# A DiT attention block on one core: x only centred for K, 1/sigma applied later, scale's first part of three blocks, w_mod by neighbouring rows

## The chip, the cores and the metric

The kernel runs on one NeuronCore of a Trainium2 chip. The core has a matrix engine (PE; its weight loads are listed apart as PEld), a vector engine (DVE), a scalar engine (ACT), a general-purpose engine (POOL) and a queue engine (SP), which here only issues transfers. ACT also issues a few. Transfers between the chip's DRAM (HBM) and the on-chip memory (SBUF) run on 16 DMA engines; matrix products land in a second on-chip memory (PSUM) of eight banks. The engines run side by side, each in its own order, and wait for one another through semaphores.

The metric is device time in microseconds of one execution. The kernel before takes 100.85 us, the median of three runs (100.76 to 101.13). Times in the text are us from the start of the profiled span unless a unit is given.

## The reference

The block is the attention half of a diffusion transformer with adaptive layer norm. B = 2 batches of N = 256 tokens, D = 1152, all bfloat16:

```
mod = (silu(c) @ w_mod).reshape(B, 6, 1, D)
shift_a, scale_a, gate_a, ... = [mod[:, i] for i in range(6)]
h = layernorm(x) * (1 + scale_a) + shift_a
q, k, v = split(h @ wqkv)
p = softmax(q @ k.T * D ** -0.5)
out = x + gate_a * ((p @ v) @ wo)
```

Three of the six modulation vectors are used: shift, scale and gate. `layernorm(x)` is `(x - mean) / sigma` per token, so 1/sigma is one number per token. Adding the same vector to every key adds, for one query, the same number to all its scores, which the softmax removes; so the shift may be left out of K.

## The kernel before, in words

D is cut into KT = 9 blocks of 128 and the 512 tokens into TT = 4 tiles of 128 (tiles 0 and 1 are batch 0, tiles 2 and 3 batch 1). Every engine's order is written out by hand: `vec`, `sca`, `ten` and `spq` record each DVE, ACT, PE and SP instruction (they all show as line L74 in the profile), and `pin` at the end fixes each engine's recorded order. POOL's instructions are not recorded and stand in program order. So the order of the source text is the order on each engine.

**Loads.** SP issues all weights and x in one sequence (L138 to L153): x tiles 1, 0, 3; the first KA x 128 columns of scale's weights (`wS`) in pairs of row blocks; K's rows 0 to KA - 1 (first 1024 columns, one row block each, with x tile 2 after the first); the rest of scale's columns; the rest of K's rows; K's last 128 columns of the first rows; shift's weights `wH`. Later come Q's and V's weights in chunks of 384 columns (`wqv`), the gate's weights `wG` and `wo`. c goes by ACT's queue (L118).

**c and the modulation.** c is loaded as 18 rows of 128 (L115, L118), turned by PE into `cT_ps` (L157), put through silu with one exponential on ACT and three DVE steps (`silu_c`, L170), and copied 27 times over by ACT into `scT_rep`, since a product with a few more columns is no dearer for PE. `scale_A`, `scale_B` and `shift_block` multiply blocks of `wS` and `wH` with it: scale's first KA = 4 blocks into `psSA` and `psS0` (which are started from ones, for 1 + scale), the other five into `psSB`, shift into `psH`. Twelve products on a constant (`fillers`, L160) run ahead of this on PE, seven more (`fillers2`, L256) between the first scale products and transposes.

**Layer norm.** For tiles 1, 0 and 2, DVE takes statistics (`dve_stats`, `dve_aggr`), POOL adds eps and raises to the power -0.5, DVE makes `nb` = -mean/sigma and then `xn` = x * rstd + nb in one step (`dve_norm`). For tile 3, ACT takes mean and variance (`act_mean`, `act_var`). PE turns `xn` block by block (`transposes`) and DVE or ACT copies the result to `xnT` (features on partitions, tokens along the row).

**K first.** K needs no shift, so it starts before shift is known: `scaled` (DVE) multiplies a block of `xnT` by 1 + scale into `hTs`; `k_part` adds a block of K's rows to six open accumulators (`accs`, one bank each, 512 tokens wide), first for batch 0 (256 columns), then tile 3, then tile 2 (128 columns each), for the first KA blocks; `early_half` does the same for two more output blocks, into `psE` and from there into `early`. Then come `scale_B`, `scaled` for the other blocks, and `k_step` for these with 512 columns. The accumulators are copied to `qkT` by DVE and ACT in turn (`evac`). Shift's products follow, with `k_block` for the remaining output blocks between them; DVE adds `early` to two of these, copies `psH` to `sh`, and `modulated` (DVE and ACT) makes `hT` = xnT * (1 + scale) + shift, the input of Q and V.

**Then** Q (nine blocks of nine products), the scores, softmax (`row_max`, `exps`, `normalized`), V, attention times V, and the output projection with the gate. The gate is summed on DVE in 18 steps (`gate_step`, `gacc`), reduced over partitions on POOL (`gate_bc`, L558), and POOL multiplies it into the last columns of `wo` (`wo_last`, L579), which PE's last products read.

Of the kernel before, what the change touches and what calls it, by code (L numbers as in the profile page):

```python
# [7 lines left out]
ACT = mybir.ActivationFunctionType  # L8
# [8 lines left out]
def kernel(  # L17
# [9 lines left out]
    nc = tc.nc  # L27
# [14 lines left out]
    KA = 4  # L42
# [6 lines left out]
    wmod_v = w_mod.rearrange("(kk p) (s n) -> p kk s n", p=P, s=6)  # L49
# [45 lines left out]
    def tok(b):  # L95
        return slice(b * N, (b + 1) * N)
# [13 lines left out]
    neg_half = const.tile([P, 1], F32)  # L110
# [4 lines left out]
    c_sb = const.tile([2 * KT, P], BF16)  # L115
    x_sb = act.tile([P, TT, D], BF16)
    nc.scalar.preload_act_table_set("natural_log_exp_and_others")
    nc.scalar.dma_start(out=c_sb, in_=c.rearrange("b (k p) -> (b k) p", p=P))  # L118
# [8 lines left out]
    def load_x(t):  # L127
        spq.dma_start(out=x_sb[:, t, :], in_=x_f[t * P : (t + 1) * P, :])

    def load_mod(tile_, which, k0, k1, c0, c1):  # L130
        spq.dma_start(out=tile_[:, k0:k1, c0:c1], in_=wmod_v[:, k0:k1, which, c0:c1])

    def load_k(k0, k1, c0=0, c1=D):
        spq.dma_start(out=wK[:, k0:k1, c0:c1], in_=wqkv_v[:, k0:k1, D + c0 : D + c1])
# [8 lines left out]
    load_k(0, 1, 0, WE)  # L143
    load_x(2)
    for k in range(1, KA):
        load_k(k, k + 1, 0, WE)
    load_mod(wS, 1, 0, 5, CA, D)
    load_mod(wS, 1, 5, KT, CA, D)
    load_k(KA, 6)
    load_k(6, KT)  # L150
# [5 lines left out]
    cT_ps = psum_b.tile([P, 2 * KT], BF16, tag="pb")  # L156
    ten.transpose(cT_ps, c_sb, ident[: 2 * KT, : 2 * KT])  # L157
    junk_ps = psum_a.tile([P, 512], F32, tag="pa")

    def fillers(n):  # L160
        for _ in range(n):
            ten.matmul(junk_ps, lhsT=ident, rhs=junk_rhs, start=True, stop=True)

    fillers(12)
    e_sb = small.tile([P, 2 * KT], F32, tag="e_sb")
    sca.activation(out=e_sb, in_=cT_ps, func=ACT.Exp, scale=-1.0)
# [3 lines left out]
    def silu_c():  # L170
        vec.tensor_scalar_add(out=e_sb, in0=e_sb, scalar1=1.0)
        vec.reciprocal(out=e_sb, in_=e_sb)
        vec.tensor_tensor(
            out=scT_f.rearrange("p k b -> p b k"),
            in0=cT_ps.rearrange("p (b k) -> p b k", b=B),
            in1=e_sb.rearrange("p (b k) -> p b k", b=B),
            op=ALU.mult,
        )
        sca.copy(out=scT_rep, in_=scT_f.unsqueeze(2).to_broadcast([P, KT, NR // B, B]))
# [5 lines left out]
    mv_all = const.tile([P, TT, 2], F32)  # L185
    rstd = const.tile([P, TT], F32)
    nb = const.tile([P, TT], F32)
    xn = act.tile([P, TT, D], BF16, tag="a1")
    xnT = act.tile([P, KT, T], BF16, tag="a2")
    stats = {t: small.tile([P, NCH, 6], F32, tag="stats", name="stats") for t in (1, 0, 2)}  # L190

    def dve_stats(t, s):
        vec.bn_stats(out=stats[t][:, s, :], in_=x_sb[:, t, s * CW : (s + 1) * CW])

    def dve_aggr(t):
        vec.bn_aggr(out=mv_all[:, t, :], in_=stats[t])
        nc.gpsimd.tensor_scalar_add(out=rstd[:, t : t + 1], in0=mv_all[:, t, 1:2], scalar1=EPS)
        nc.gpsimd.tensor_tensor(out=rstd[:, t : t + 1], in0=rstd[:, t : t + 1], in1=neg_half, op=ALU.pow)  # L198

    def dve_nb(t):  # L200
        vec.scalar_tensor_tensor(
            out=nb[:, t : t + 1], in0=mv_all[:, t, 0:1], scalar=-1.0, in1=rstd[:, t : t + 1],
            op0=ALU.mult, op1=ALU.mult,
        )

    def dve_norm(t):
        vec.tensor_scalar(
            out=xn[:, t, :], in0=x_sb[:, t, :], scalar1=rstd[:, t : t + 1], scalar2=nb[:, t : t + 1],
            op0=ALU.mult, op1=ALU.add,
        )  # L210

    ssum = small.tile([P, 1], F32, tag="ssum")
    nmean = small.tile([P, 1], F32, tag="nmean")
    ssq = small.tile([P, 1], F32, tag="ssq")

    def act_mean(t):
        sca.activation(out=xn[:, t, :], in_=x_sb[:, t, :], func=ACT.Copy, accum_out=ssum)
        sca.activation(out=nmean, in_=ssum, func=ACT.Copy, scale=-1.0 / D)

    def act_var(t):  # L220
        sca.activation(out=xn[:, t, :], in_=x_sb[:, t, :], func=ACT.Square, bias=nmean,
                       scale=1.0, accum_out=ssq)
        nc.gpsimd.tensor_scalar(out=rstd[:, t : t + 1], in0=ssq, scalar1=1.0 / D, scalar2=EPS,
                                op0=ALU.mult, op1=ALU.add)
        nc.gpsimd.tensor_tensor(out=rstd[:, t : t + 1], in0=rstd[:, t : t + 1], in1=neg_half, op=ALU.pow)
        nc.gpsimd.tensor_tensor(out=nb[:, t : t + 1], in0=nmean, in1=rstd[:, t : t + 1], op=ALU.mult)

    tps = {}
    HALF = ((0, KA), (KA, KT))

    def transposes(t, h, pool, tag):
        k0, k1 = HALF[h]
        tp = pool.tile([P, KB, P], BF16, tag=tag, name="tp")
        for k in range(k0, k1):
            ten.transpose(tp[:, k - k0, :], xn[:, t, k * P : (k + 1) * P], ident)
        tps[t, h] = tp

    def xnT_copy(t, h, on_dve):
        k0, k1 = HALF[h]
        dst, srct = xnT[:, k0:k1, t * P : (t + 1) * P], tps[t, h][:, : k1 - k0, :]  # L240
        if on_dve:
            vec.tensor_copy(out=dst, in_=srct)
        else:
            sca.copy(out=dst, in_=srct)

# [4 lines left out]
    hT = act.tile([P, KT, T], BF16)  # L250
    qkT = act.tile([P, 2 * KT, T], BF16)
    early = const.tile([P, NEARLY, T], F32)

    junk_mm = psum.tile([P, 512], F32, tag="mm")

    def fillers2(n):  # L256
        for _ in range(n):
            ten.matmul(junk_mm, lhsT=ident, rhs=junk_rhs, start=True, stop=True)
# [8 lines left out]
    def scale_A(kk):  # L267
        for j in range(KA):
            ten.matmul(
                psS0 if j == 0 else psSA[:, j - 1, :], lhsT=wS[:, kk, j * P : (j + 1) * P], rhs=sc_rhs(kk),  # L270
                start=False, stop=(kk == KT - 1), skip_group_check=True,
            )
# [15 lines left out]
    def one(t):  # L288
        return slice(t * P, (t + 1) * P)
# [11 lines left out]
    def early_half(k, b, ps):  # L301
        for i in range(NEARLY):
            ten.matmul(
                ps[:, i, :], lhsT=wK[:, k, (NACC + i) * P : (NACC + i + 1) * P], rhs=hTs[:, k, tok(b)],
                start=(k == 0 and i == 0), stop=(k == KA - 1), skip_group_check=True,
            )
# [19 lines left out]

    silu_c()
    for s in range(NCH):
        dve_stats(1, s)
    dve_aggr(1)  # L330
    for s in range(NCH):
        dve_stats(0, s)
    dve_aggr(0)
    act_mean(3)
    dve_nb(1)
    dve_norm(1)
    dve_nb(0)
    dve_norm(0)
    scale_A(0)
    fillers2(2)  # L340
    scale_A(1)
    fillers2(2)
    transposes(1, 0, psum, "mm")
    transposes(1, 1, psum, "mm")
    xnT_copy(1, 0, False)
    xnT_copy(1, 1, False)
    fillers2(3)
    scale_A(2)
    scale_A(3)
    transposes(0, 0, psum, "mm")  # L350
    transposes(0, 1, psum, "mm")
    xnT_copy(0, 0, True)
    xnT_copy(0, 1, True)
    act_var(3)
    for kk in range(4, KT):
        scale_A(kk)

# [8 lines left out]
    early_half(0, 0, psE)  # L366
    k_part(1, tok(0))
    early_half(1, 0, psE)
    dve_stats(2, 0)
    dve_norm(3)  # L370
    k_part(2, tok(0))
    transposes(3, 0, psum_b, "pb")
    xnT_copy(3, 0, False)
    k_part(3, tok(0))
    dve_stats(2, 1)
    dve_stats(2, 2)
    dve_aggr(2)
    for k in range(KA):
        scaled(k, one(3), s1p[:, k, 1:2])
    transposes(3, 1, psum_b, "pb")  # L380
    xnT_copy(3, 1, False)
    early_half(2, 0, psE)
    for k in range(KA):
        k_part(k, one(3))
    dve_nb(2)
    dve_norm(2)
    transposes(2, 0, psum_b, "pb")
    xnT_copy(2, 0, True)
    early_half(3, 0, psE)
    sca.copy(out=early[:, :, tok(0)], in_=psE)  # L390
    transposes(2, 1, psum_b, "pb")
    xnT_copy(2, 1, False)
    for k in range(KA):
        scaled(k, one(2), s1p[:, k, 1:2])
    for k in range(KA):
        k_part(k, one(2))
    psSB = psum_a.tile([P, KB, NR], F32, tag="pa")
    for kk in range(KT):
        scale_B(kk)
# [7 lines left out]
    sca.copy(out=early[:, :, tok(1)], in_=psE)  # L407

# [4 lines left out]
    for f in range(NACC):  # L413
        evac(f, qkT[:, KT + f, :], accs[f])
# [92 lines left out]
    def row_max(b):  # L507
        mx = small.tile([P, NQ], F32, tag="mx")
        vec.reduce_max(out=mx, in_=s_tiles[b], axis=AX.X)
        nmxs[b] = small.tile([P, NQ], F32, tag="nmx", name="nmx")  # L510
        vec.tensor_scalar_mul(out=nmxs[b], in0=mx, scalar1=-SM_SCALE)

    def exps(b):
        p_fs[b] = work.tile([P, NQ, N], F32, tag="p_f", name="p_f")
        rsums[b] = small.tile([P, NQ], F32, tag="rsum", name="rsum")
        for i in range(NQ):
            sca.activation(
                out=p_fs[b][:, i, :], in_=s_tiles[b][:, i, :], func=ACT.Exp,
                bias=nmxs[b][:, i : i + 1], scale=SM_SCALE, accum_out=rsums[b][:, i : i + 1],
            )  # L520
# [142 lines left out]
```

## Time and profile before

| what | value |
|---|---|
| median of three runs | 100.85 us (100.76 to 101.13) |
| profiled execution: its own time, its span | 101.4 us, 99.5 us |
| PE, DVE, ACT, POOL busy | 92.7, 66.8, 29.3, 24.5 us |
| DMA | 21.06 MB, 326 to 414 GB/s in the slices from 7.5 to 54.7 us |
| first K product on PE | 12.62 |
| last product of shift, first product of Q | 33.4, 35.3 |
| scores on PE | 52.8 to 56.7 |
| last product on PE, output done | 94.8, 99.5 |

The profile is of one execution, whose own time (101.4) is 0.55 above the median of the runs; the span is from the first to the last instruction. A busy engine is not by itself the limit: the chain of waits, which follows back from the last instruction to what released it, tells which work set the end. A wait that is listed as "engine tile <- engine tile: total, times, longest" names the engine that stood idle first, and what ended its wait behind the arrow.

### The profile page before, as it was taken

How to read it: one execution, taken by the hardware profiler on the slowest of the kernel's cores; microseconds unless marked ns; L12 is line 12 of the kernel's file. 1: busy time of each engine (PE TensorE's matmuls, PEld its weight loads, DVE VectorE, ACT ScalarE, POOL GpSimd, SP SyncE). 2: the span in 40 equal slices, each digit the busy share in tenths (PEclk: the TensorE clock that was granted, in tenths of full speed). 3: DMA queues.
4: the chain of work that ended last, by engine and by line, in shares of the span. 5: the costliest groups of instructions: out<-in, count | busy, mean ns of one | idle time of the engine just before them, and what ended most of it. 6: DMA issues, size and time to landing. Idle time of an engine off the chain costs nothing.

```text
span 99.5 us, 1843 instructions
## 1 busy us (share of the span) xinstructions
PE 92.7 (93%) x753; PEld 57.3 (58%) x753; DVE 66.8 (67%) x131; ACT 29.3 (29%) x58; POOL 24.5 (25%) x29
## 2 busy tenths in 40 slices
PE   0899999899999999999999999999999999999960
PEld 0334788894465644444447866566568766556560
DVE  1694398426063899999992999960237767879870
ACT  5340905402060494223322453323126400000000
POOL 5042043000000000000000000039999910079600
PEclk9999999999999999999999999999999999999999
DMA  2999999999999999999999300000000000302212
GB/s 59 319 259 368 403 395 407 386 394 414 382 370 389 359 403 377 342 326 327 347 410 412 127 0 0 0 0 0 0 0 10 0 0 0 119 5 114 88 70 85
DMA packets 16339, 21.06 MB, mean 212 GB/s; under 512 B 1355, under 2 KB 10827, under 8 KB 16331
## 3 DMA queue, kind: packets, MB, share of 16 engines
q1 hardware_dynamic: 16160, 20.93, 59.7%
q8 instruction: 6, 0.10, 0.4%
q10 hardware_dynamic: 171, 0.02, 0.1%
q14 instruction: 2, 0.02, 0.0%
HBM read 19.76 MB, written 1.18 MB: 210 GB/s over the span
## 4 chain that ended last, share of the span: by engine, by line
PE 86%; DVE 6%; DMA 2%; POOL 1%; issue 1%; ACT 0%; DVEq 0%
PE ps L74 59%; PE acc L74 12%; PE s_ps L74 4%; DVE stats L74 3%; PE tp L74 2%; PE psH L74 2%; DMA c_sb<-in_c_dram 2%; PE psE L74 2%; PE junk_mm L74 2%; PE psSB L74 1%; PE psSA L74 1%; DVE o_sb L74 1%; DVE ga L74 1%; POOL rstd L198 1%; DVE mv_all L74 0%
## 5 line engine op out<-in xcount | busy, mean ns | idle before, releaser
L558 POOL PARTITION_ALL_REDUCE gate_bc<-gacc x2 | 13.7, 6886 | 49.8 <-DVE gacc L74 49.8
L74 DVE SCALAR_TENSOR_TENSOR gacc<-wG,scT_f,gacc 128x1152 f32<-128x1152 bf16 x16 | 22.7, 1418 | 0.5
L74 PE MATMUL ps<-wqv,hT 128*128 128x384 bf16 x108 | 17.9, 326 | 0.0
L74 PE MATMUL ps<-hT,wqv 128*128 128x512 bf16 x81 | 17.6, 379 | 0.0
L74 PE MATMUL ps<-wO,attnT 128*128 128x384 bf16 (+1 forms) x108 | 17.0, 319 | 0.0
L74 PEld LDWEIGHTS <-attnT 128*128 128x128 bf16 x126 | 11.3, 98 | 6.4
L74 PEld LDWEIGHTS <-hT 128*128 128x128 bf16 x108 | 10.5, 98 | 6.7
L74 PEld LDWEIGHTS <-wK 128*128 128x128 bf16 x137 | 11.1, 97 | 5.8 <-issue 0.5
L74 PEld LDWEIGHTS <-wqv 128*128 128x128 bf16 x81 | 7.9, 98 | 9.6 <-DVE hT L74 0.4
L74 PE MATMUL acc<-hTs,wK 128*128 128x128 bf16 (+2 forms) x102 | 12.9, 278 | 0.4 <-DVE hTs L74 0.4
L74 ACT CAST qkT<-ps 128x512 bf16<-128x512 f32 x10 | 5.8, 583 | 10.9 <-PE ps L74 10.9
L74 DVE TENSOR_TENSOR ga<-ps,gate_bc 128x384 f32<-128x384 f32 (+1 forms) x12 | 6.5, 540 | 3.4 <-PE ps L74 3.4
L579 POOL TENSOR_TENSOR wo_last<-wO,gate_bc 128x192 bf16<-128x192 bf16 x9 | 5.9, 683 | 7.6 <-issue 7.6
L74 ACT CAST v_sb<-ps 128x384 bf16<-128x384 f32 x10 | 4.8, 478 | 9.6 <-PE ps L74 9.6
L74 DVE TENSOR_TENSOR o_sb<-ga,x_sb 128x384 bf16<-128x384 f32 (+1 forms) x12 | 7.3, 609 | 0.4
L74 PE MATMUL junk_ps<-junk_rhs,ident 128*128 128x512 bf16 x12 | 5.3, 632 | 0.0
L74 ACT CAST o_sb<-ps 128x64 bf16<-128x64 f32 x1 | 0.2, 212 | 17.3 <-PE ps L74 17.3
L74 DVE CAST v_sb<-ps 128x384 bf16<-128x384 f32 x2 | 1.1, 557 | 6.0 <-PE ps L74 6.0
L74 ACT COPY xnT<-tp 128x640 bf16<-128x640 bf16 (+1 forms) x5 | 3.1, 650 | 6.0 <-PE tp L74 6.0
L74 DVE CAST attnT<-ps 128x512 bf16<-128x512 f32 (+1 forms) x6 | 3.5, 603 | 1.8 <-PE ps L74 1.8
L74 DVE CAST qkT<-acc 128x512 bf16<-128x512 f32 x3 | 1.9, 685 | 4.1 <-PE acc L74 4.1
L74 PE MATMUL ps<-hTs,wK 128*128 128x512 bf16 x19 | 4.6, 378 | 0.0
(77 smaller groups left out, 89.7 us busy)
## 6 DMA issues: line engine op xcount, KB each, us to landing
wqv<-in_wqkv_dram SPq DMA_DIRECT2D x5, 864.0 KB, 12.1
wG<-in_w_mod_dram SPq DMA_DIRECT2D x3, 864.0 KB, 10.5
wO<-in_wo_dram SPq DMA_DIRECT2D x3, 864.0 KB, 9.2
wH<-in_w_mod_dram SPq DMA_DIRECT2D x4, 576.0 KB, 9.9
x_sb<-in_x_dram SPq DMA_DIRECT2D x4, 288.0 KB, 3.3
wS<-in_w_mod_dram SPq DMA_DIRECT2D x4, 256.0 KB, 5.9
wK<-in_wqkv_dram SPq DMA_DIRECT2D x4, 256.0 KB, 6.0
wK<-in_wqkv_dram SPq DMA_DIRECT2D x1, 864.0 KB, 10.4
```

What stands on the lines that cost most here:

```text
L74: r = fn(*a, **k)
L198: nc.gpsimd.tensor_tensor(out=rstd[:, t : t + 1], in0=rstd[:, t : t + 1], in1=neg_half, op=ALU.pow)
L558: ar = nc.gpsimd.partition_all_reduce(gate_bc[:, b, :], gacc[:, b, :], P, bass.bass_isa.ReduceOp.add)
L579: nc.gpsimd.tensor_tensor(out=wo_last[:, k, :], in0=wO[:, k, D - TAILW :], in1=gate_bc[:, B - 1, D - TAILW :], op=ALU.mult)
```

## The change

Four things change together.

- **x is only centred for K.** `xn` becomes `xc` = x - mean (`centre`, DVE). 1/sigma of a key's token multiplies all its scores with every query, so it is applied to the scores: `row_max` multiplies the score tile by `rstd_bc`, a row of the 512 tokens' 1/sigma that is the same on all partitions, into `p_f`, and the maximum and the exponentials read `p_f`. For Q and V, nine DVE products multiply `xnT` in place by `rstd_bc`, after K's `scaled` steps and before `hT`. 1/sigma is formed for all four tiles at once on POOL, written to a small DRAM tensor with tokens in order (`rstd_out`), and read back as a row to all partitions (`rstd_in`); both transfers go by ACT's queue, the second after the first has landed.
- **Statistics are shared out anew.** DVE takes tiles 1 and 3 (tile 3's variance late, its mean early on ACT), ACT means and variances of 0 and 2. Tiles 3 and 2 are each turned with eight blocks in one go, and the ninth blocks of both later, between `scale_B` steps.
- **KA is 3 instead of 4**: scale's first part has three blocks, K starts with three blocks of rows, and six remain for `k_step`. All six accumulators are copied by ACT.
- **w_mod and c by neighbouring rows.** Partition p takes rows 9p to 9p + 8 of `w_mod` instead of rows p, p + 128, and so on; c comes in the same order straight onto the partitions, without PE's transpose. The 13 first fillers no longer wait for c; `fillers2` is gone but for two.

SP issues K's second row block ahead of x tile 2, the rest of scale's columns in three transfers and the rest of K's rows in pairs.

```diff
-    KA = 4
+    KA = 3
-    wmod_v = w_mod.rearrange("(kk p) (s n) -> p kk s n", p=P, s=6)
+    wmod_v = w_mod.rearrange("(p kk) (s n) -> p kk s n", p=P, s=6)
-    nc.scalar.dma_start(out=c_sb, in_=c.rearrange("b (k p) -> (b k) p", p=P))
+    nc.scalar.dma_start(out=c_sb, in_=c.rearrange("b (p k) -> p b k", p=P))
...
     load_k(0, 1, 0, WE)
+    load_k(1, 2, 0, WE)
     load_x(2)
-    for k in range(1, KA):
-        load_k(k, k + 1, 0, WE)
-    load_mod(wS, 1, 0, 5, CA, D)
-    load_mod(wS, 1, 5, KT, CA, D)
-    load_k(KA, 6)
-    load_k(6, KT)
+    load_k(2, 3, 0, WE)
+    for k0 in range(0, KT, 3):
+        load_mod(wS, 1, k0, k0 + 3, CA, D)
+    for k0 in range(KA, KT, 2):
+        load_k(k0, k0 + 2)
...
-    ten.transpose(cT_ps, c_sb, ident[: 2 * KT, : 2 * KT])
...
-    fillers(12)
+    fillers(13)
...
+    def var_eps(t):
+        nc.gpsimd.tensor_scalar(out=rstd[:, t : t + 1], in0=mv[:, t, 1:2], scalar1=1.0, scalar2=EPS,
+                                op0=ALU.mult, op1=ALU.add)
     def act_mean(t):
+        sca.activation(out=xc[:, t, :], in_=x_sb[:, t, :], func=ACT.Copy, accum_out=sums[:, t, 0:1])
+        sca.activation(out=mv[:, t, 0:1], in_=sums[:, t, 0:1], func=ACT.Copy, scale=1.0 / D)
     def act_var(t):
+        sca.activation(out=square, in_=xc[:, t, :], func=ACT.Square, accum_out=sums[:, t, 1:2])
...
+    def centre(t, c0=0, c1=D):
+        vec.tensor_scalar(out=xc[:, t, c0:c1], in0=x_sb[:, t, c0:c1], scalar1=mv[:, t, 0:1], scalar2=None,
+                          op0=ALU.subtract)
+    def rstd_out():
+        nc.gpsimd.tensor_tensor(out=rstd, in0=rstd, in1=neg_half, op=ALU.pow)
+        sca.dma_start(out=sigma_dram.rearrange("t p -> p t"), in_=rstd)
+    def rstd_in():
+        flat = sigma_dram.rearrange("t p -> (t p)")
+        sca.dma_start(out=rstd_bc, in_=flat.unsqueeze(0).to_broadcast([P, T]))
...
+    dve_stats(1, 0)
     silu_c()
-    for s in range(NCH):
-        dve_stats(1, s)
+    dve_stats(1, 1)
+    dve_stats(1, 2)
     dve_aggr(1)
+    centre(1)
+    var_eps(1)
+    act_mean(0)
+    centre(0)
     act_mean(3)
...
     k_part(0, tok(0), first=True)
     early_half(0, 0, psE)
+    centre(3, CW, D)
     k_part(1, tok(0))
+    act_mean(2)
+    tp3 = bank(n=KT - 1, pool=psum_b, tag="pb")
+    turned(tp3, tiles_of(3, 0, KT - 1))
...
+    tp2 = bank(n=KT - 1, pool=psum_b, tag="pb")
+    turned(tp2, tiles_of(2, 0, KT - 1))
+    from_psum(vec, 2, 0, KA, tp2)
     for k in range(KA):
         scaled(k, one(2), s1p[:, k, 1:2])
+    from_psum(sca, 2, KA, KT - 1, tp2, KA)
+    for s in range(NCH):
+        dve_stats(3, s)
+    dve_aggr(3)
+    var_eps(3)
     for k in range(KA):
         k_part(k, one(2))
-    for kk in range(KT):
+    for kk in range(6):
+        scale_B(kk)
+    tp8 = bank(n=2, pool=psum_b, tag="pb")
+    turned(tp8, [(3, KT - 1), (2, KT - 1)])
+    from_psum(vec, 3, KT - 1, KT, tp8, 0)
+    from_psum(vec, 2, KT - 1, KT, tp8, 1)
+    rstd_out()
+    for kk in range(6, KT):
         scale_B(kk)
...
     sca.copy(out=early[:, :, tok(1)], in_=psE)
+    rstd_in()
+    for k in range(KT):
+        vec.tensor_tensor(out=xnT[:, k, :], in0=xnT[:, k, :], in1=rstd_bc, op=ALU.mult)
...
-        evac(f, qkT[:, KT + f, :], accs[f])
+        evac(1, qkT[:, KT + f, :], accs[f])
...
     def row_max(b):
+        vec.tensor_tensor(out=p_fs[b], in0=s_tiles[b], op=ALU.mult,
+                          in1=rstd_bc[:, tok(b)].unsqueeze(1).to_broadcast([P, NQ, N]))
-        vec.reduce_max(out=mx, in_=s_tiles[b], axis=AX.X)
+        vec.reduce_max(out=mx, in_=p_fs[b], axis=AX.X)
```

## The prediction

> **What bounds the kernel now.** I read the chain of waits first, then PE's own waits, the timeline around the places the diff touches, and the transfers. All times are of the one profiled execution: span 99.5, 101.4 us in all, 0.55 above the median of the runs (100.85).
>
> The chain of waits in order of time (start, us, what):
> ```profile
> 0.76 2.00 DMA c_sb<-in_c_dram
> ...
> 8.29 0.31 PE psSA L74
> ...
> 12.27 0.30 DVE hTs L74
> ...
> 12.62 0.82 PE acc L74 x6
> ...
> 16.73 1.34 PE acc L74 x24
> ...
> 20.60 1.15 PE psSB L74 x45
> ...
> 22.63 6.54 PE acc L74 x30
> ...
> 32.47 0.91 PE psH L74 x36
> 33.38 19.43 PE ps L74 x90
> 52.80 3.93 PE s_ps L74 x36
> ```
> From 12.62, when the first K product starts, PE is the chain almost without a break until 94.76. PE's waits, all of them, behind that point come to 0.3:
> ```profile
> PE cT_ps L74 <- DMA c_sb<-in_c_dram: 2.8, 1, 2.8
> PE acc L74 <- DVE hTs L74: 0.4, 1, 0.4
> PE tp L74 <- DVE xnT L74: 0.3, 1, 0.3
> ```
> So the end is the start of K (I call it S, 12.62 now) plus PE's work plus its holes. Q's first product now starts at 35.32 (33.38 + 9 x 0.216); behind that the work is the same in both kernels. The only tight place in between is the hand-over to Q, seen in the timelines of DVE and of PE's weight loads:
> ```profile
> 33.42 0.18 DVE L74 COPY sh<-psH 128x18 f32<-128x18 f32 x1 [0.22 <-PE psH L74]
> 33.63 3.17 DVE L74 TENSOR_SCALAR hT<-xnT,s1p,sh 128x256 bf16<-128x256 bf16 x12
> 36.85 1.21 PEld L74 LDWEIGHTS <-wqv 128*128 128x128 bf16 x7 [0.16 <-DVE hT L74]
> ```
> Q chases hT with no slack: any delay of `sh` or hT on DVE delays Q one for one. The loads ahead of S (DMA view, windows around 4.1 and 4.7 us) and two DVE prices (groups):
> ```profile
> wS<-in_w_mod_dram SPq DMA_DIRECT2D x1, 128.0 KB, 6.2
> wK<-in_wqkv_dram SPq DMA_DIRECT2D x1, 256.0 KB, 6.4
> L74 DVE CAST qkT<-acc 128x512 bf16<-128x512 f32 x3 | 1.9, 685 | 4.1 <-PE acc L74 4.1
> L74 DVE TENSOR_TENSOR qkT<-ps,early 128x512 bf16<-128x512 f32 x2 | 1.4, 692 | 1.8 <-PE ps L74 1.8
> ```
>
> **1. The start S.** Now the last part of scale's first half is issued near 4.12 and lands at 10.3, and K's first rows (issued 4.63) at 11.0; yet K starts at 12.62. What holds it is the compute in front: statistics of two tiles on DVE to 7.2, two powers on POOL (0.67 each), norms, transposes, and seven fillers of PE (1.5 us in the chain from 8.91). The change removes c's transpose on PE, three of the four POOL powers, the `nb` steps (three on DVE, one on POOL) and five of those seven fillers; the 13 others need only DVE's memset (0.91 + 0.48), so they run from about 1.45 at 0.43 each (the twelve of now: 2.92 to 8.28, less the latency of the last) to 7.0. Walk through the new front: x tile 1 lands 0.73 + 3.0 = 3.7; one bn_stats 0.47 (1.40/3) to 4.2; silu 0.65 to 4.9; two more and the aggregate to 6.05; `centre(1)` 0.58 to 6.6. ACT: scT_rep 0.59 to 5.5, `act_mean(0)` 1.16 + 0.19 + 0.20 to 7.1; `centre(0)` to 7.7; copies of 384 and 768 columns (0.42 for 512, 0.48 for 640: I take 0.36 and 0.55) to 8.6; tile 0 turned and copied by 9.3. c itself now comes in 256 runs of 18 bytes instead of 18 of 256: landing 2.75 at best, 4.3 if each of 16 runs per engine waits behind an x packet; the chain above has that much room. Tile 3's mean on ACT (7.1 to 8.7) and its centring on DVE (0.2 + 0.4) stand beside this, behind tile 0's. So compute is ready at 9.3 and the loads decide. Three blocks instead of four are 288 KB less; at the 260 to 372 GB/s of the slices from 5 to 10 us that is 0.8 to 1.1 us: scale's first part at 9.4, K's rows at 10.1. The new row order of w_mod changes which rows one transfer touches; I find no row that prices it, and take 0, between 0.9 lost and 0.5 won. S = 10.4, ends 9.9 to 11.3: **2.2 earlier**.
>
> **2. PE from S to Q.** Columns are the same, cut otherwise. By the chain's rows (256 columns 0.109, 128 columns 0.056, 512 columns 0.216, 54 columns 0.0255): 18 + 12 of 256, 36 + 18 of 128, 54 + 81 of 54, 36 + 12 + 9 of 512 make 3.27 + 3.02 + 3.44 + 12.3 = 22.05, plus 0.16 for the first fill. Before it is 35.32 - 12.62 = 22.70 with the 0.3 wait. New holes: tile 2 is now turned in one go with nothing behind it, so PE waits for latency 0.2, copy 0.36, `scaled` 0.2 and gaps, less five transposes: 0.6 to 0.9. Behind scale's second part, s1p and two `scaled` (0.2 + 0.17 + 0.44) are covered by only 0.65 of `early_half`: 0.2. Together 23.25, **0.6 given back**. Q could start at 33.65, psH end at 31.7.
>
> **3. The loads beside it.** SP issues the same bytes; x tile 2 goes behind one K row (lands about 11.7 as now), K's rest, which lands by 21.4 now (11.04 + 10.4), comes in pairs at about 18.5, 20 and 21.4 against uses at 19.2, 21.8 and 24.4; wH's last, 28.6 now (18.39 + 10.2), against 31.0; wqv's first 29.4 against 33.65. The DMA engines are saturated to 55 us, so an earlier PE eats 1.7 of slack, and the new 256 KB broadcast and 512 pieces of 4 bytes take up to 1 more; each still fits. Cost 0; if K's first pair is late, 0 to 0.5. One coupling is new: the two queues share a rotation of semaphores, and in the changed order SP's first wqv load waits for the 4-byte write of part 4 and its first wG load for the broadcast. SP reaches these at 19.2 and 24.0 now, with loads up to 33.3 in flight (24.02 + 9.3 for wG itself), so a hold until 25 starves nothing; one beyond 29 would.
>
> **4. 1/sigma's row.** New work on DVE between `scaled` and `qkT+early`: nine products 128x512 with a float32 operand. From the three casts, (1.89 - 0.685) / 2 = 0.60 apart, 0.69 for the last: 5.5 us (ends 4.8 by the 0.264 spacing of 256 columns of hT, 6.2 by 0.69 each). They have room: DVE is busy for 1.88 of the 5 us from 25 to 30, and most of that are the three `acc` casts, which leave for ACT (three more of 0.59; six end by 30.0, and k_block(7) needs only the first). `scaled` ends about 21.6 (12 x 0.22 from 18.9); then DVE waits for rstd_bc, and behind that wait stand both adds, `sh` and hT. When does the row land? Tile 2 is turned at S + 4.2 = 14.6; its copy and three `scaled` to 16.0; tile 3's statistics, moved here, 1.4 + 0.24 to 17.65; POOL 0.23 and the power 0.63 with handovers to 18.7. ACT, which waits here with one copy and the `acc` casts of 26 behind it, then issues the write of 512 pieces of 4 bytes. Low end: c's 2.0 from issue to landing, 20.7. High end: 32 pieces per engine, each behind a weight packet (2304 bytes at 25 GB/s per engine, 0.092): 2.9 more, 23.6. Only then does ACT issue the read of 128 x 2 KB: low 2.0 (c) to 2.1 (the output's 288 KB), high 3.0 (x's first) + 0.7 of sharing. rstd_bc lands at **22.7 to 27.3; I take 24.5**, near the low end, since the page's q10 line (171 small packets, 0.1% of 16 engines) makes a small packet about 9 ns and nothing shows one waiting. Products end at 30.0, the adds (0.65 each) at 31.3, before psH at 31.7: cost 0, with 0.4 to spare. No landing after 24.9 is free.
>
> The Trainium skill ("DMA: Bandwidth & Descriptors", "Queues, rings and completion order") says that an engine goes round its queues, taking a packet of 9 to 17 descriptors at a turn; by it ACT's pieces need two to four turns, and the estimate is a landing near 23. The same page ("Specifications") sets 512 bytes as the least size at line rate, with read-modify-write below it; that speaks against the write of 4-byte pieces, and no row here prices it.
>
> **5. Scores and gate.** Two more DVE products (0.69 each) ahead of the row maxima, in a stretch where DVE is 4.86 and 4.89 of 5 busy: gacc ends 1.4 later relative to PE. It ends now at 66.3; POOL then works without a break until wo_last ends at 93.58 (87.71 + 5.87), needed at about 95.25: slack 1.67 less 1.4. Cost 0, barely.
>
> **Sum:** 2.2 - 0.6 = 1.6 us earlier; 101.4 - 1.6 = 99.8 for the profiled execution, 100.85 - 1.6 = **99.3** against the median.
>
> **The rivals.** (a) Slower: rstd_bc lands late. From 24.9 each us costs one; at 26.5 the gain is gone; at 27.3 with products of 0.69 the loss is 1.5 (102.4); if the 4-byte writes themselves take longer still, 28.5 costs 2 to 2.7 (about 103). For it: two transfers in series behind a saturated stream. Against: small packets at 9 ns. (b) The new row order loads scale's part later: S 11.3 to 12.5, gain 0.1 to 0.7, 100.2 to 100.8. For it: only 260 GB/s in the slice where w_mod's first rows come. (c) The gate ends late: if the two products cost 0.9 each with their handovers, or gacc loses 0.5 elsewhere, PE waits up to 0.6 for wo_last, 99.9. For it: a slack of 0.3; against: only sums of small terms. (d) PE's pace: the first 12 fillers ran 0.43 apart and the next ones 0.215; with PE partly idle from 7.0 to 10.4 the faster pace could come late and cost about 1.7 in K's parts (3.4 us at half pace): 101. For it: the faster pace came only at 8.7, behind 5.8 us without a hole. Against: between 7.0 and 10.4 there are still 18 transposes, 27 scale products and 2 fillers.
>
> **How the numbers follow.** Forecast 0.52, its own range 98.5 to 100.0 (S 9.9 to 11.3, a landing up to 25.5). (a), a landing after that, 0.28, of which 0.04 ends within 0.5% (about what a measurement of this kernel can tell from no change). (b) 0.10, half of it within. (c) 0.06. (d) 0.04, within. Faster 0.52 + 0.05 + 0.06 = 0.63; same 0.04 + 0.05 + 0.04 = 0.13; slower 0.24. Low 98.5; the high end goes to 102.0, which leaves out the worst part of (a), about 0.12, as the low end leaves out some 0.06.
>
> **What would show it.** First `acc` product at 10.4, with PE waiting for wS or wK ahead of it; a wait of 0.6 to 0.9 on hTs ahead of the last K part; DVE's first xnT product at 24.5 (a long wait there, and Q's first product later than 33.7, is rival a); psH ending near 31.7; wo_last ending just before PE asks. Wrong if Q starts after 35.3.

## The result

| | before | after |
|---|---|---|
| median of 4 runs, us | 100.92 (100.76 to 101.13) | 113.41 (111.81 to 113.61) |
| profiled execution: its own time, its span | 101.4, 99.5 | 111.81, 109.9 |
| mean granted clock of PE | 1.000 | 0.953 |
| first K product | 12.62 | 9.48 |
| first product of Q | 35.32 | 44.38 |
| scores | 52.80 | 63.36 |

The ratio of the times is 1.115, with a 95% interval of 1.1022 to 1.1279 (two disturbed executions of the four after are left out of it, so it is not the quotient of the two medians). The forecast was 99.3 with a range up to 102.0: wrong in sign and far outside.

The chain of waits of the kernel after (start, us, what):
```profile
9.48 0.81 PE acc L74 x6
...
14.61 0.58 DVE hTs L74 x3
15.19 1.40 DVE stats L74 x3
...
17.21 1.13 POOL rstd L236
...
18.36 13.12 DMA sigma_dram<-rstd
...
31.51 5.26 DMA rstd_bc<-sigma_dram
...
37.41 4.90 DVE xnT L74 x8
...
44.38 18.98 PE ps L74 x81
63.36 3.93 PE s_ps L74 x36
```
Before, PE carried the chain from 12.62 on. Now it leaves PE at the turning of tile 2 and runs over DVE and POOL to two transfers, which together hold it for 18.4 us: 2048 bytes out, in 13.12, and 256 KB back, in 5.26. The K products start 3.1 earlier than before, and Q starts 9.1 later. From Q to the scores PE takes 18.98 us for 81 products (17.48 before), which makes the scores 10.56 later; behind them everything takes what it took, to within 0.2.

What stood idle meanwhile, from the list of waits (total, times, longest):
```profile
DVE xnT L74 <- DMA rstd_bc<-sigma_dram: 16.5, 1, 16.5
ACT qkT L74 <- DMA sigma_dram<-rstd: 12.6, 1, 12.6
...
PE ps L74 <- ACT hT L74: 6.5, 1, 6.5
...
PE psH L74 <- DMA wH<-in_w_mod_dram: 2.4, 2, 2.2
```
DVE waits for the row, ACT waits with it (the read is queued on ACT behind the write's landing), and PE, out of work, waits 6.5 for `hT`. The last line is a second effect: shift's weights came late too. The page's slices show why (each is 2.75 us):
```profile
PEclk9999999999959985599999999999999999999999
...
GB/s 82 303 355 382 376 379 389 367 371 108 113 33 210 323 352 362 390 356 328 299 336 333 402 342 29 0 0 0 0 0 0 0 6 0 62 45 107 0 107 107
```
In slices 10 to 12 (24.7 to 33), from 6 us after the write's issue to just behind its landing, the whole weight stream falls from some 370 to 108, 113 and 33 GB/s. (SP waits 9.4 for the write too and issues nothing from 22.1 to 31.5; the last of the three may owe something to that.) The last of shift's weights lands at 35.5 (28.6 before); of these 6.9 us, 3.3 are its later issue (21.72, 18.39 before), and 3.6 its longer way (13.8, 10.2 before). PE's granted clock falls twice around its idle stretches.

What the DMA engines do in the meantime, by queue, in the windows 18.4 to 22.2 (first line) and 22.2 to 31.5 (packets, MB, the time of the packets as a share of 16 engines; q1 is SP's queue, q10 ACT's; 528 packets are the 512 pieces and 16 landing signals):
```profile
q1 hardware_dynamic: 999, 1.40, 106.9%
...
q1 hardware_dynamic: 725, 1.57, 106.0%
q10 hardware_dynamic: 528, 0.00, 3.4%
```
In the first window ACT's queue has no packet at all: the first piece goes out some 4 us after the write was issued. In the second the engines are as busy with weights as before, but 1.57 MB take 9.3 us where 1.40 MB took 3.8. So over most of this time the engines do not lack loads; the packets take longer.

So two things go with the write: it takes 13.1 us itself, and the weights nearly stop. The experiments ask which of its properties does this, and whether the rest of the change is worth anything.

### The profile page after: what moved, and what is told of

Same layout as the page of the kernel before. It is cut to its first block, busy times and chain, and to the rows that moved or that the text cites. A ratio compares the mean times of both kernels' runs of the same rounds, so it can differ in the third digit from the quotient of the medians.

```text
span 109.9 us, 1819 instructions
## 1 busy us (share of the span) xinstructions
PE 95.0 (86%) x734; PEld 57.1 (52%) x734; DVE 70.1 (64%) x136; ACT 33.4 (30%) x67; POOL 23.1 (21%) x25
## 4 chain that ended last, share of the span: by engine, by line
PE 67%; DMA 17%; DVE 10%; issue 1%; POOL 1%; ACT 1%; DVEq 0%; ACTq 0%
PE ps L74 51%; DMA sigma_dram<-rstd 12%; PE junk_ps L74 5%; DVE xnT L74 5%; DMA rstd_bc<-sigma_dram 5%; PE s_ps L74 4%; PE acc L74 3%; PE tp L74 2%; DVE stats L74 1%; DVE qkT L74 1%; POOL rstd L236 1%; DVE o_sb L74 1%; DVE hTs L74 1%; DVE ga L74 1%; PE psE L74 1%
## 5 line engine op out<-in xcount | busy, mean ns | idle before, releaser
L74 PE MATMUL ps<-hT,wqv 128*128 128x512 bf16 x81 | 19.0, 399 | 6.5 <-ACT hT L74 6.5
L74 DVE TENSOR_TENSOR xnT<-xnT,rstd_bc 128x512 bf16<-128x512 bf16 x9 | 5.5, 686 | 16.5 <-DMA rstd_bc<-sigma_dram 16.5
L74 PEld LDWEIGHTS <-wK 128*128 128x128 bf16 x123 | 10.4, 99 | 8.9 <-issue 2.3
L74 PE MATMUL acc<-hTs,wK 128*128 128x128 bf16 (+2 forms) x90 | 12.6, 294 | 1.3 <-DVE hTs L74 1.1
L74 PE MATMUL junk_ps<-junk_rhs 128*128 128x512 bf16 x15 | 5.9, 566 | 1.4 <-DVE junk_rhs L74 1.4
L74 ACT CAST qkT<-acc 128x512 bf16<-128x512 f32 x6 | 3.0, 613 | 12.6 <-DMA sigma_dram<-rstd 12.6
L74 PE MATMUL ps<-hTs,wK 128*128 128x512 bf16 x21 | 6.3, 452 | 0.2 <-ACT qkT L74 0.2
L74 ACT ACTIVATE hT<-xnT,sh,s1p 128x256 bf16<-128x256 bf16 x6 | 3.1, 587 | 8.7 <-DVE sh L74 8.7
L74 PE MATMUL psH<-scT_rep,wH 128*128 128x54 bf16 x81 | 3.3, 191 | 2.4 <-DMA wH<-in_w_mod_dram 2.4
## 6 DMA issues: line engine op xcount, KB each, us to landing
wH<-in_w_mod_dram SPq DMA_DIRECT2D x4, 576.0 KB, 12.6
wK<-in_wqkv_dram SPq DMA_DIRECT2D x3, 576.0 KB, 10.7
```

What stands on the lines that cost most here:

```text
L74: r = fn(*a, **k)
```

## The experiments

Kernels for which no ratio is given ran once each, and that one execution is the profiled one.

### The row without DRAM

First, undo one thing only: make the same row on PE. 1/sigma on a diagonal (two bfloat16 parts, so that nothing is lost), times a matrix of ones, is the row on all partitions.

```diff
-        sca.dma_start(out=sigma_dram.rearrange("t p -> p t"), in_=rstd)
-    def rstd_in():
-        flat = sigma_dram.rearrange("t p -> (t p)")
-        sca.dma_start(out=rstd_bc, in_=flat.unsqueeze(0).to_broadcast([P, T]))
+    def diags():
+        vec.tensor_copy(out=rstd_hi, in_=rstd)
+        vec.tensor_tensor(out=rstd_lo, in0=rstd, in1=rstd_hi, op=ALU.subtract)
+        for j, src in enumerate((rstd, rstd_lo)):
+            for t in range(TT):
+                vec.tensor_scalar(out=diag[:, j, t, :], in0=ident, scalar1=src[:, t : t + 1], scalar2=None,
+                                  op0=ALU.mult)
+    def row_on_pe():
+        for j in range(2):
+            ten.matmul(row_ps, lhsT=ones_bf, rhs=diag[:, j].rearrange("p t n -> p (t n)"),
+                       start=(j == 0), stop=(j == 1))
+        sca.copy(out=rstd_bc, in_=row_ps)
...
-    rstd_in()
+    diags()
+    for k in range(KA, KA + 2):
+        k_step(k)
+    row_on_pe()
```

> The changed kernel with 1/sigma's row made on the chip: POOL's power as before, then DVE puts 1/sigma on diagonals (a high and a low bfloat16 part), two products of PE with ones spread it over the partitions, ACT copies it to rstd_bc. No write to DRAM and no read back; all else is as in the changed kernel. Theory A (the loss is the two transfers of the row): the row is there near 23 to 24 instead of 36.8, DVE's nine products end near 29.5, Q starts at 33.0 to 33.4, the kernel takes 98.3 to 99.2. Theory B (the loss lies in the rest of the change: more work on DVE, the new row order of w_mod, PE's clock): it stays above 102.

Measured: 100.42 us against 101.07, ratio 0.9942 (0.9906 to 0.9978); span 98.6 in the profiled execution (97.9 to 98.8 in the others). The round trip is the loss: without it 109.9 becomes 98.6. But the gain is less than expected. PE's waits:
```profile
PE acc L74 <- DVE hTs L74: 0.7, 1, 0.7
PE acc L74 <- DVE s1p L74: 0.4, 1, 0.4
PE row_ps L74 <- DVE diag L74: 0.3, 1, 0.3
PE acc L74 <- DMA wK<-in_wqkv_dram: 0.2, 1, 0.2
```
K starts at 9.53 (the wait for `s1p` is ahead of it), Q at 34.5 (by the chain, as in the forecast: 32.53 + 9 x 0.216): 24.95 between them, where the forecast had 23.25. The row costs 1.16 of the 1.7: the twelve `k_step` products ahead of it, from 18.80 at 0.216 each, are done at 21.39, and the next starts at 22.55. Only 0.43 of that is the two row products; during the other 0.73 PE waits for the diagonals, which DVE makes too late. The waits for tile 2's `scaled` (0.74) and K's rows (0.24) are about the 1.0 that the forecast had for holes.

### Is it the pieces? Four writes that nobody reads

The same 512 pieces of 4 bytes, put into the kernel before and read by nobody, once amid the weights and once late, when no other transfer runs:

```diff
...
+    sca.dma_start(out=sigma_dram.rearrange("t p -> p t"), in_=rstd)   # before_write: ahead of tile 2's K parts
...
+    sca.dma_start(out=sigma_dram.rearrange("t p -> p t"), in_=rstd)   # before_write_quiet: behind V's groups
```

> The kernel before with one more transfer and nothing else: ACT writes 1/sigma as 512 pieces of 4 bytes to a scratch tensor near 20, in the middle of the weights; nobody reads it. Theory A1: it takes 10 to 14 us, the weights behind it come late (shift's last rows at 33 to 36 instead of 28.6), and the kernel takes 103 to 108. Theory A2: it takes as long, but the weights keep their pace, and the kernel stays within 101 to 102.

> As the last, but the write is issued near 72, when no other transfer runs. Theory A1 with the price in DRAM alone: still 5 us or more from issue to landing. If the price comes only from meeting the weights: 2 to 3 us. The kernel stays at 100.5 to 101.5 either way.

Measured: 105.4 and 100.21, beside medians of 101.07. Amid the weights, from the transfers issued around 19.4 (last column: us from issue to landing), and from the page's slices:
```profile
wH<-in_w_mod_dram SPq DMA_DIRECT2D x1, 288.0 KB, 16.3
sigma_dram<-rstd ACTq DMA_DIRECT2D x1, 2.0 KB, 12.6
```
```profile
GB/s 83 303 257 377 401 395 409 372 406 361 127 58 20 289 397 363 396 392 339 327 326 349 410 409 94 0 0 0 0 0 6 3 0 0 114 0 114 63 61 110
```
The write alone makes a kernel that does not need it 4 us slower, with the same dip in the stream (127, 58, 20) and shift's last weights 16.3 us under way (10.2 before). PE waits 2.0 for them. In the quiet, the transfers issued in a window around 70.4, and then the window from 71.2 to 79 in 40 slices:
```profile
sigma_dram<-rstd ACTq DMA_DIRECT2D x1, 2.0 KB, 8.3
```
```profile
GB/s 0 6 5 0 0 0 0 0 0 0 0 0 0 84 0 0 0 0 0 0 0 0 42 0 0 0 0 0 0 0 0 0 0 0 0 0 0 0 0 0
...
q10 hardware_dynamic: 528, 0.00, 3.2%
```
The pieces are sent in two slices, from 71.4 to 71.8 (the later two spikes are larger packets of other queues), yet the landing is at 78.8. So even with no load beside it the write takes 8.3 us, seven of them after the last piece has left. This price comes behind the sending: a count of pieces and turns, as the forecast made it, cannot see it.

Next, what about the pieces does it? First, larger ones, in the changed kernel: each partition's four numbers side by side, 128 pieces of 16 bytes. The row then holds the numbers in another order than the tokens, so this kernel leaves out the right pairing of 1/sigma with tokens; the work is the same.

```diff
-        [TT, P], F32, name="sigma_dram")
+        [P, TT], F32, name="sigma_dram")
...
-        sca.dma_start(out=sigma_dram.rearrange("t p -> p t"), in_=rstd)
+        sca.dma_start(out=sigma_dram, in_=rstd)
...
-        flat = sigma_dram.rearrange("t p -> (t p)")
+        flat = sigma_dram.rearrange("p t -> (p t)")
```

> The changed kernel, but the scratch tensor has 1/sigma in the order of the partitions, so that the write is 128 pieces of 16 bytes side by side instead of 512 pieces of 4 bytes; the row that is read back then has the tokens in another order, so the output leaves out the right order of 1/sigma. Theory A1 (each small piece has its price in DRAM): the write takes about 3.3 (13.1 x 128/512) plus 2 us instead of 13.1, and the kernel 103 to 106. Theory A2 (any transfer of ACT's queue waits behind the weights, whatever its pieces): 12 to 13 us again, 112 to 114.

Measured: 105.58. The write took 6.1 us and the read 5.8, so the row landed at 30.2 instead of 36.8, 6.6 earlier, and the time is 6.2 below that of after's profiled execution. The stream's smallest slice is 239 GB/s: the stall is much smaller. Fewer and larger pieces do help, but number, size and neighbourhood all changed at once. So three writes in the quiet, in the kernel before, again read by nobody: (a) 128 pieces of 16 bytes; (b) 512 pieces of 4 bytes, each in 64 bytes of its own; (c) 512 pieces of 4 bytes side by side.

```diff
+    sig_a = dram.tile([P, TT], F32, name="sig_a")
+    sig_b = dram.tile([TT, P, 16], F32, name="sig_b")
+    sig_c = dram.tile([TT, P], F32, name="sig_c")
...
+        if gidx == 0:
+            sca.dma_start(out=sig_a, in_=rstd)
+        if gidx == 4:
+            sca.dma_start(out=sig_b.rearrange("t p s -> p t s")[:, :, 0], in_=rstd)
+    sca.dma_start(out=sig_c.rearrange("t p -> p t"), in_=rstd)
```

> The kernel before with three writes of 1/sigma that nobody reads, one after the other in the stretch where no other transfer runs: (a) 128 pieces of 16 bytes side by side near 59, (b) 512 pieces of 4 bytes, each in 64 bytes of its own, near 65, (c) the 512 pieces of 4 bytes side by side as in the change, near 72. Theory C1 (pieces that share a stretch of DRAM wait for one another): (a) 2 to 3 us from issue to landing, (b) 2 to 3, (c) 8. Theory C2 (each small piece has its price, wherever it goes): (a) 3.5 to 4, (b) 8, (c) 8. Where ACT's waits do not show a landing, the DMA view or SP's waits for the semaphores do.

Measured (100.9, as the kernel before), the transfers issued around 58.1 and 63.9:
```profile
sig_a<-rstd ACTq DMA_DIRECT2D x1, 2.0 KB, 1.4
...
sig_b<-rstd ACTq DMA_DIRECT2D x1, 2.0 KB, 2.1
```
(c) was sent by 72.6. The view gives it no landing, but 14 of its 16 landing signals are on record, between 77.45 and 79.72, the last some 8.5 us after its issue at 71.2. Between (b) and (c) the pieces have the same number and size, and differ in place: 2.1 against 8.5. So smallness alone does not do it. Neighbourhood alone does not either: the pieces of (a) lie side by side too, four to 64 bytes, and took 1.4. What is dear is many pieces of 4 bytes side by side. That they wait for one another, each rewriting the same stretch of DRAM, is what fits; it was argued, not shown, and how long such a stretch is was not measured ((c) lies in 2 KB, (b) over 32 KB). One difference between (b) and (c) is not excluded here: POOL reduces the gate from 66.2 to 79.9, beside (c) and not beside (b). The next pair of writes is free of it.

Does the same property hold up the weights? The write amid the weights once more, each piece in 64 bytes of its own:

```diff
-        [TT, P], F32, name="sigma_dram")
+        [TT, P, 16], F32, name="sigma_dram")
...
-    sca.dma_start(out=sigma_dram.rearrange("t p -> p t"), in_=rstd)
+    sca.dma_start(out=sigma_dram.rearrange("t p s -> p t s")[:, :, 0], in_=rstd)
```

> As before_write (512 pieces of 4 bytes written near 20, amid the weights), but each piece in 64 bytes of its own. Theory: what costs is that neighbouring pieces share a stretch of DRAM; the wait for the write behind the weights (3.7 to its first piece) stays, but it lands 5 to 6.5 after issue instead of 12.6, the weights keep their pace (shift's last rows by 29 to 30 instead of 35.4), and the kernel takes 100.8 to 101.8 instead of 105.4. Rival (512 small pieces amid the weights cost as such): 104 to 106 again.

Measured: 101.25 beside 100.85 (105.4 side by side). The page's slices and the transfers around 19.2:
```profile
GB/s 54 322 276 361 402 394 406 385 393 398 372 369 390 354 403 382 341 326 326 345 406 409 171 0 0 0 0 0 0 0 10 0 0 0 119 0 119 83 65 97
```
```profile
wH<-in_w_mod_dram SPq DMA_DIRECT2D x1, 288.0 KB, 9.7
sigma_dram<-rstd ACTq DMA_DIRECT2D x1, 2.0 KB, 8.6
```
No dip: the stream holds 354 to 403 GB/s where it had fallen to 20, and shift's last weights land on time. Only the place of the pieces differs between the two kernels, so 4-byte pieces side by side are what stalls the stream. The write itself still took 8.6 us, more than expected: ACT's queue has no packet from 19.3 to 22.5, and the pieces are sent between 22.5 and 27.9. Even well placed pieces are slow beside the weights. (The changed kernel itself with spaced pieces was not run.)

### Would one piece be enough?

Take the pieces away but keep DRAM: the row made on PE as above, written as one row of 2 KB and read back to all partitions.

```diff
-        sca.copy(out=rstd_bc, in_=row_ps)
+        sca.copy(out=row_sb, in_=row_ps)
+        flat = sigma_dram.rearrange("t p -> (t p)").unsqueeze(0)
+        sca.dma_start(out=flat, in_=row_sb[0:1, :])
+        sca.dma_start(out=rstd_bc, in_=flat.to_broadcast([P, T]))
```

> As row_on_pe, but the row made on PE goes to DRAM as one piece of 2 KB and comes back as the broadcast of the change. Theory: two things make the changed kernel's round trip slow, the small pieces and that each transfer of ACT's queue first waits 2 to 4 us behind weights already in the engines. Then the write takes 4 to 5 us (3.9 to its first packet and a normal landing), the read 5, the row is there near 32 to 33 and the kernel takes 104 to 106. If the pieces alone were to blame: 2 and 3 us, the row near 28.5, 101.5 to 102.5.

Measured: 109.71. The chain:
```profile
22.99 3.88 DMA sigma_dram<-row_sb
...
26.95 6.26 DMA rstd_bc<-sigma_dram
...
40.80 20.36 PE ps L74 x81
```
A clean round trip still costs 10.1 us. Its write has no packet among those moved from 23.0 to 26.3 (719 of SP's queue, none of ACT's), and its first in the window from 26.3 to 26.95:
```profile
q1 hardware_dynamic: 719, 1.31, 102.6%
...
q10 hardware_dynamic: 2, 0.00, 0.9%
```
(the first line is of the earlier window, the second of the later; q10 is the queue that ACT issues to). The read, issued at 26.95, likewise shows none of its own until after 30.7. So a transfer on ACT's queue waits over 3 us before its first packet, a time that SP's packets fill; why it waits so long is not shown. The round trip was priced about right: the row came at 33.2, where 32 to 33 was expected. The expectation missed in what follows from there. With the row at 30.2, `pieces16` took 105.58, so 3.0 later gives 108.6 and not 104 to 106; and PE, idle, then took 20.36 for the 81 products that took 17.48 before, at a mean granted clock of 0.968.

### Does PE's lost pace matter in the changed kernel?

28 products on a constant, whose result nobody uses, ahead of Q in the changed kernel keep PE busy through the wait:

```diff
+    junk_q = psum.tile([P, 512], F32, tag="mm", name="junk_q")
+    for _ in range(28):
+        ten.matmul(junk_q, lhsT=junk_rhs[:, 0:P], rhs=junk_rhs, start=True, stop=True)
     for f in range(KT):
         wt, off = chunks_w[f * P // CW], f * P % CW
```

> The changed kernel with 28 products on a constant, put on PE just ahead of Q's first product, where PE stood idle from 37.5 to 44.4. They do no work for the result. Theory: of the changed kernel's loss a part is PE's pace, which fell to half because PE stood idle; kept busy, Q's 81 products take 17.5 instead of 19.0 and the kernel 110.0 to 110.8 by the same start of Q, 1.4 to 1.9 less than 111.8. Rival: the pace of Q's first products is set by something else (hT coming piece by piece): 111.5 to 112.

Measured: 111.5, ratio 1.1051 (1.0983 to 1.112). The chain, and then the same place:
```profile
38.03 4.88 DVE xnT L74 x8
...
46.94 16.44 PE ps L74 x75
63.38 3.93 PE s_ps L74 x36
```
Q's products now run at full pace (16.44/75 = 0.219 each), the row came 0.6 later than in the profile of after, and the scores start at the same 63.4. So the lost pace cost after some 0.6 us; the remainder of the slower Q is PE following `hT` block by block. The expected gain was missed, and the ratio's interval overlaps that of the changed kernel: the row sets the time.

### The new row order of w_mod, alone

```diff
-    wmod_v = w_mod.rearrange("(kk p) (s n) -> p kk s n", p=P, s=6)
+    wmod_v = w_mod.rearrange("(p kk) (s n) -> p kk s n", p=P, s=6)
-    nc.scalar.dma_start(out=c_sb, in_=c.rearrange("b (k p) -> (b k) p", p=P))
+    nc.scalar.dma_start(out=c_sb, in_=c.rearrange("b (p k) -> p b k", p=P))
```

> The kernel before with the row order of w_mod and c alone: partition p takes rows 9p to 9p + 8, c comes in that order without PE's transpose; KA stays 4. If the order of the rows made the early loads faster (in the changed kernel scale's first part landed at 8.7 instead of 10.3, of which three blocks for four explain 0.8 to 1.1), they land at 9.4 to 9.9 here; if not, at 10.2 to 10.5. The kernel's time hangs on compute up to 12.6, not on these loads: 100.3 to 101.1, no difference to be measured, but for the earlier silu.

Measured: 101.43 against 100.92, ratio 1.0061 (1.0029 to 1.0093). The chain's start:
```profile
0.75 2.92 DMA c_sb<-in_c_dram
...
12.53 0.81 PE acc L74 x6
```
Scale's first part landed at 9.87 (10.35 in the profile of before, 10.06 in that of the kernel with the extra write), so the order gains a few tenths at most; c, in 256 runs of 18 bytes, takes 2.92 instead of 2.00. No difference was expected, and the 0.6% is clear of noise. But K's start is the same within 0.1, and so is the span (99.4, 99.5 before), so the profile does not show where the 0.6% goes: that stays open.

### The version without the round trip, tuned

Two of the holes of the first experiment can be filled: two `scale_B` blocks go ahead of tile 2's K parts, into the wait of 0.7, and the diagonals go ahead of the last eight `scaled` steps. In a second step ACT's copy to `early` goes ahead of tile 2's variance, since the first step had left PE a wait of 0.7 for it.

```diff
+    for kk in range(2):
+        scale_B(kk)
     for k in range(KA):
         k_part(k, one(2))
-    for kk in range(6):
+    for kk in range(2, 6):
         scale_B(kk)
...
     for k in range(KA, KT):
+        if k == KA + 2:
+            diags()
...
-    diags()
```

> The row made on PE once more, with two holes of PE closed that the last trace showed: the diagonals are made ahead of eight of the `scaled` steps (PE had waited 0.7 for them between K steps), and two blocks of scale's second part stand in the hole of 0.7 between tile 2's transposes and its K parts. Theory: what the early start gains is given back in PE's holes, so closing 1.1 to 1.4 us of them shows in full: 99.0 to 99.6 where row_on_pe took 100.4, ratio to the kernel before 0.980 to 0.987. Rival: the gate's chain (DVE's gacc, POOL's reduction, wo_last) has become the bound and takes it away: 100.2 to 100.5 again.

```diff
-    act_var(2)
     sca.copy(out=early[:, :, tok(0)], in_=psE)
+    act_var(2)
```

> row_tuned with one more exchange: on ACT the copy of `early` for batch 0 goes ahead of tile 2's variance, because in row_tuned's trace PE stood 0.7 idle until that copy freed the bank of scale's second part. Theory: PE's holes between S and Q are the bound, so the time falls by another 0.4 to 0.7: 98.9 to 99.2, ratio to the kernel before 0.980 to 0.986. Rival: the variance, now 0.6 later, delays 1/sigma's row or tile 2's copies, and the time stays at 99.4 to 99.7.

Measured: 99.58, ratio 0.9894 (0.9855 to 0.9933), and then 99.52, ratio 0.986 (0.9813 to 0.9907): faster than both kernels. The first step's median is just inside what was expected (99.0 to 99.6), its ratio just outside. The second step missed its 98.9 to 99.2 and came out where its rival had it: PE's wait for `early` fell from 0.7 to 0.2, but the medians differ by 0.06, so its gain is not clear of noise. PE's last waits in its list (the first of them is ahead of the first K product), and the chain, of the second:
```profile
PE acc L74 <- DVE hTs L74: 0.3, 1, 0.3
PE psSB L74 <- ACT early L74: 0.2, 1, 0.2
```
```profile
9.90 0.81 PE acc L74 x6
...
21.22 0.43 PE row_ps L74 x2
...
31.47 19.42 PE ps L74 x90
50.90 3.93 PE s_ps L74 x36
```
PE is the chain again from 9.90 on. Q starts at 33.41 (31.47 + 9 x 0.216), 23.51 after K, of which 0.43 is the row; the scores start 1.9 earlier than before.

## Why the prediction was wrong, step by step

**1, the start: right in direction, better than said.** S was 9.48, not 10.4. The loads that were to decide landed at 8.68 (scale's first part; 9.4 forecast) and 9.37 (K's first row; 10.1); compute, forecast at 9.3, was ready just behind. c came at 3.98, inside its bounds (2.75 to 4.3). Rival (b) fell: the row order loses nothing on scale's part. (Its worst case did not follow from the forecast's own sum: S at 12.5, 0.1 earlier than before, less the 0.6 of step 2, is a loss of 0.5 and not a gain of 0.1.)

**2, PE from S to Q: 0.5 short.** It cannot be read from after, where PE waited for the row. Where the row is made on PE it is 24.95 - 1.16 = 23.8 without the row, against 23.25. The holes were as said (0.74 behind tile 2's turning, forecast 0.6 to 0.9, and 0.24 for K's rows, forecast 0 to 0.5); it is the bare work that takes 22.8, not the 22.2 of the column sum, which leaves out the short steps between groups. With the holes filled, the tuned version has 23.51 - 0.43 = 23.08.

**3, the loads: failed at one place, with its condition stated.** K's pairs landed at 18.6, 20.1 and 21.7 (forecast 18.5, 20, 21.4). The coupling was named: "a hold until 25 starves nothing; one beyond 29 would". The hold lasted until 31.5: SP issued the first load of `wqv` at 31.50 (19.2 before) and that of `wG` at 36.85. What was not foreseen is that loads already in flight stall too: shift's last weights landed 6.9 us later than before (half of it by their later issue), PE waited 2.4 for them, and this lay inside the longer wait for the row.

**4, the row: the step that failed.** Everything around the write was close: issue 18.36 (18.7 forecast, although the power of four columns took 1.13 and not 0.63), the nine products 5.5 in all, 0.60 apart as forecast. This group of the page has price and wait in one line:
```profile
L74 DVE TENSOR_TENSOR xnT<-xnT,rstd_bc 128x512 bf16<-128x512 bf16 x9 | 5.5, 686 | 16.5 <-DMA rstd_bc<-sigma_dram 16.5
```
The write's landing was priced at 2.0 to 4.9 us and took 13.1; the read's at 2.0 to 3.7 and took 5.3. The mis-sized term is the write's high end, "32 pieces per engine, each behind a weight packet". It counts the sending, and leaves out what comes ahead of it and behind it. Ahead: in every kernel that writes the row amid the weights, ACT's queue shows no packet of it for over 3 us (18.4 to 22.2 in after, 19.3 to 22.5 with spaced pieces, 23.0 to 26.3 for one piece). Behind: 2.1 us from issue to landing for 512 separate pieces in the quiet, 8.3 to 8.5 if they are neighbours, and 12.6 if the weights run beside them, which then nearly stop. The small packets' 9 ns on the page was taken as evidence that none waits; it says nothing of when they start or land.

So there are two parts to the 18.4 us of the round trip. As one clean piece of 2 KB it costs 10.1 behind this stream, as 128 pieces of 16 bytes 11.9; the rest, 6.5 to 8.3, goes with the 4-byte neighbours. By the first part alone the row, whose write is issued at 18.4, would land at about 28.5 (an estimate from these runs), already past the 24.9 that was free.

The Trainium skill ("DMA: Bandwidth & Descriptors", "Specifications") has the write below 512 bytes as read-modify-write. The prediction quoted that as speaking against the change and left it without a price. It pointed the right way, but does not tell the cases apart: 16-byte pieces and separate 4-byte pieces are below 512 bytes too, and took 1.4 and 2.1. The turns of the queues on the same page of the Trainium skill ("Queues, rings and completion order") gave an estimate near 23. No run bears that out for a transfer issued behind SP's loads: a single 2 KB write had no packet for 3.3 us.

Rival (a) had the right mechanism and sign, and its rule holds: "From 24.9 each us costs one". The row landed at 36.77, 11.9 past that point; the nine products that had stood between shift's end and Q (1.94 from one to the other) ran during the wait, and from `sh` to Q only 0.87 was left, which gives 1.1 back; so Q should be 11.9 - 1.1 = 10.8 later than forecast, and was 44.38 - 33.65 = 10.7. Its price, up to about 103, was capped by the same high end as the forecast, and so was the range.

**5, scores and gate: right.** In the tuned version POOL's gate starts at 65.96 (66.42 before) where PE's scores are 1.9 earlier, so 1.4 later relative to PE, as forecast, `wo_last` ends at 92.41, and PE does not wait for it. Rival (c) did not come.

**Rival (d)**, a lost pace between 7 and 10, did not come either: the granted clock of the tuned version is 1.000. Pace was lost where PE idled for the row, at a cost of some 0.6.

Against the forecast of 99.3, the change without the round trip takes 100.42 as it stands and 99.52 with its holes filled: the sum's other steps hold to about 1 us (0.9 more gained at S, 0.5 less behind it, 1.2 for the row on PE), and the two transfers made the difference of 11 us in the span.

## What to carry to other kernels

Price a round trip through DRAM from issue to landing, beside the transfers that will run: here it cost 10.1 us in the best case, and pieces of 4 bytes side by side landed later still and held up the other transfers, however little time their packets took. A row that PE can make from a diagonal in 0.43 us should not leave the chip while a weight stream runs. Where no row of a trace prices a transfer, its high end should come from the nearest bad case, not from a count of packets.

## What the runs showed that was not expected

- 512 writes of 4 bytes, nothing beside them: 2.1 us with each in 64 bytes of its own, 8.3 to 8.5 side by side, with all pieces sent in the first 1.4.
- The side-by-side write takes the stream of weights from some 370 GB/s down to 20 to 130 for about 8 us; the spaced one leaves it at 354 or more, and takes 8.6 itself.
- A transfer of ACT's queue issued amid SP's loads had no packet for over 3 us, be it one piece of 2 KB (3.88 to landing), 128 of 16 bytes (6.1), 512 of 4 bytes (8.6 spaced) or the 256 KB read (6.26); in the quiet the first packet came after about 1.
- c in 256 runs of 18 bytes lands 0.92 later than in 18 of 256.
